# Carried-state and value-key products of an mLSTM kernel cut into tiles of 32 columns

## The chip, the core and the metric

One NeuronCore of one Trainium2 chip runs the whole program. Its engines are TensorE (PE, with its weight loads shown as PEld), VectorE (DVE), ScalarE (ACT), GpSimd (POOL) and the DMA queues, which SyncE (SP) starts. The metric is device microseconds (us) of one execution. The kernel before took 723.89 us, the median of three runs from 721.53 to 728.03.

## What is computed

The program is an mLSTM attention over 4 batches, 8 heads, 768 positions and 40 dimensions a head, and behind it two dense layers on the 3072 tokens. The attention keeps a state per head:

```python
for t in range(S):
    m_new = np.maximum(f_gate[:, :, t] + m, i_gate[:, :, t])
    f_stab = np.exp(f_gate[:, :, t] + m - m_new)
    i_stab = np.exp(i_gate[:, :, t] - m_new)
    C = f_stab[:, :, None, None] * C + i_stab[:, :, None, None] * np.einsum('bhd,bhe->bhde', vt, kt)
    n = f_stab[:, :, None] * n + i_stab[:, :, None] * kt
    h_tilde = np.einsum('bhde,bhe->bhd', C, qt)
    nq = np.einsum('bhd,bhd->bh', n, qt)[:, :, None]
    y[:, :, t] = o * h_tilde / np.maximum(np.abs(nq), 1.0)
```

Then `h = x @ w_in` with a softmax-weighted activation and a layer norm, `ln @ w_out`, and a gated layer of 1536 hidden units (`silu(x @ w_gate) * (x @ w_val) @ w_out`). All inputs and the output are float32.

## The kernel before

The attention is done in chunks of 128 positions (`L`). There are 6 chunks by 4 batches, 24 units `j`, and each unit holds all 8 heads. Within a chunk the products are matrix products; between chunks the state `C[b]` is carried, with the normaliser as a 41st column of each head (`D1` = 41). The 8 heads stand in the state in three groups of 3, 3 and 2: 120 partitions hold three heads' 40 key dimensions, and a mask keeps only the blocks that belong together.

Four products of a unit stand on TensorE, all in plain float32. The profile shows two records, a weight load and a matmul each, for every float32 matmul of the program:

- `sc` (line 405): queries by keys, 8 matmuls with 40 contraction rows, laid alternately in the upper and the lower half of the array's rows;
- `pv` (line 417): the masked scores by the values. Each head's 128 output rows are cut into four pieces of 32, so 32 matmuls of 32 weight columns and 41 moving columns;
- `pi` (line 424): the queries by the carried state, added to the same PSUM bank as `pv`: 3 matmuls with 120 contraction rows, 128 weight columns, and 123, 123 and 82 moving columns. It exists in 20 of 24 units (not in the first chunk);
- `pd` (line 432): the keys by the weighted values, 3 matmuls with 128 contraction rows, 120 weight columns and the same moving columns. It exists in 20 units (not in the last chunk). `cs` on VectorE masks its result, and `cd`/`ca` add it to the state.

Behind a unit's attention come, for its 128 tokens, `xT` (transposes, line 485), `h` (line 508), a softmax and a norm on VectorE and ScalarE, `uT` (transposes, line 554), `o` (line 571) and `x2` (transposes, line 485). The last layer follows (`gv`/`o2`, lines 749 to 794), from about 262 us to the end; in it a matmul uses 64 rows of the array.

Every engine executes its instructions in the order in which the program lists them. That order is written out by hand: the table `ORDER` names each step with its unit, as in `pv:8 ... pi:8`. So what stands before and behind each `pi` and `pd` on TensorE is fixed, and differs from unit to unit.

Of the kernel before, what the change touches and what calls it, by code (L numbers as in the profile page):

```python
# [19 lines left out]
L = 128  # L20
# [125 lines left out]
def kernel(  # L146
# [20 lines left out]
    D3 = 3 * D  # L167
    KF = FF // 128
    KF2 = w2.shape[0]
    act, dve, pool, pe, sp = nc.scalar, nc.vector, nc.gpsimd, nc.tensor, nc.sync  # L170
# [9 lines left out]
    def bank1():  # L180
        return psC.tile([128, 512], F32, tag="c", name="c")
# [47 lines left out]
    C, cols, gdr, edr, dend = {}, {}, {}, {}, {}  # L229
# [4 lines left out]
    def heads(a, p=128):  # L234
        return a[0:p, 0:H * D1].rearrange("p (h e) -> p h e", h=H)
# [184 lines left out]
    def pi(j):  # L420
        if j >= B:
            po, qt, b = T["pv", j], T["qT", j], j % B
            for g in range(3):
                pe.matmul(heads(po)[:, g::3, :], qt[:, g, :], C[b][:, g::3, :], start=False, stop=g == 2)  # L424

    def pd(j):
        kn = T["k", j]
        if j // B < NC - 1:
            pd_ = T["pd", j] = bank1()
            t = T["vw", j]  # L430
            for g in range(3):
                pe.matmul(heads(pd_, D3)[:, g::3, :], kn[:, g, :], t[:, g::3, :], start=True, stop=True)

    def th(j):
        T["th", j] = ak.tile([128, H, D], F32, tag="th", name="th", bufs=2)
# [538 lines left out]
```

## Time and profile before

| | |
|---|---|
| median of 3 runs | 723.89 us (721.53 to 728.03) |
| the profiled execution | 723.04 us |
| its span, first to last instruction | 721.0 us |
| TensorE busy | 696.8 us (97%) |
| VectorE busy | 450.2 us (62%) |
| ScalarE, GpSimd busy | 325.8 us (45%), 158.3 us (22%) |
| mean granted TensorE clock | 0.973 of full |

A matmul's busy time reaches from its start to the arrival of its result, so neighbours overlap, and a busy TensorE is not yet one at its peak. What an operation costs on a full TensorE is read from the distance between the start of its first record and the start of the next operation's first.

### The profile page before, as it was taken

To read this page: it belongs to the slowest core of one execution; us is meant where nothing else is said; L and a number is where in the kernel's file an instruction comes from. 1 tells how busy PE (TensorE), PEld (TensorE's weight loads), DVE (VectorE), ACT (ScalarE), POOL (GpSimd) and SP (SyncE) were. 2 spreads that over 40 slices of the span, in tenths; PEclk is the share of its full clock that TensorE was granted. 3 is DMA by queue.
4 is the path that set the end of the run, shared out by engine and by line. 5 is a ranking of instruction groups with operands and counts; after the bars stand their busy time and mean duration, and the time that the engine had idled before them with its cause. 6 is when DMAs were issued, how large, how long until landed. Compare 5 with 4: busy or idle time off the path is not lost.

```text
span 721.0 us, 16647 instructions
## 1 busy us (share of the span) xinstructions
PE 696.8 (97%) x7024; PEld 622.6 (86%) x7024; DVE 450.2 (62%) x765; ACT 325.8 (45%) x675; POOL 158.3 (22%) x230
## 2 busy tenths in 40 slices
PE   6898999999999999999999999999999999999997
PEld 6777888989999888888978888888888888888887
DVE  6999998867676696677997334344434443533433
ACT  4656757574746566567554322233222222323222
POOL 4555563624341112114235200000000000000000
PEclk8578999999999999999999999999999999999999
DMA  7897657544531042030430000010010001001001
GB/s 272 279 279 226 217 180 228 195 163 149 163 106 51 10 161 106 0 110 1 139 136 0 12 27 1 2 37 2 1 37 2 1 2 37 2 1 39 1 2 37
DMA packets 24011, 61.59 MB, mean 85 GB/s; under 512 B 3163, under 2 KB 11456, under 8 KB 23936
## 3 DMA queue, kind: packets, MB, share of 16 engines
q1 hardware_dynamic: 23936, 60.52, 26.1%
q8 instruction: 55, 0.90, 0.5%
q14 instruction: 20, 0.16, 0.1%
HBM read 56.40 MB, written 4.11 MB: 84 GB/s over the span
## 4 chain that ended last, share of the span: by engine, by line
PE 77%; DVE 11%; DMA 4%; ACT 3%; issue 2%; POOL 2%; SPq 0%; DVEq 0%; POOLq 0%; ACTq 0%
PE a L794 26%; PE c L794 14%; PE c L571 10%; PE a L508 9%; PE a L749 7%; PE c L779 3%; PE a L405 2%; PE a L554 2%; DMA kvo<-in_kvo_dram 2%; PE c L417 1%; PE c L485 1%; DVE e L521 1%; PE c L424 1%; DMA ed<-erow 1%; DMA W<-gd 1%
## 5 line engine op out<-in xcount | busy, mean ns | idle before, releaser
L794 PE MATMUL a<-Xh,w 64*128 64x512 f32 (+1 forms) x1100 | 180.2, 387 | 0.0
L757 DVE SCALAR_TENSOR_TENSOR t<-t,a 128x512 f32<-128x512 f32 x71 | 48.8, 688 | 142.6 <-ACT t L753 142.5
L794 PEld LDWEIGHTS a<-Xh,w 64*128 64x128 f32 x1100 | 101.1, 184 | 12.0 <-issue 0.2
L753 ACT ACTIVATE t<-a 128x512 f32<-128x512 f32 x71 | 42.4, 597 | 151.2 <-PE a L794 129.5
L794 PE MATMUL a<-Xl,w 64*128 64x512 f32 (+1 forms) x550 | 107.7, 382 | 0.0
L794 PE MATMUL c<-w,yh 64*128 64x320 f32 x896 | 100.5, 304 | 0.0
L794 PEld LDWEIGHTS c<-w,yh 64*128 64x128 f32 x896 | 81.4, 184 | 6.9
L765 ACT ACTIVATE yh<-t 128x512 fp32r<-128x512 f32 x71 | 44.8, 632 | 88.0 <-DVE t L761 86.8
L769 DVE TENSOR_TENSOR yl<-t,yh 128x512 fp32r<-128x512 f32 x63 | 44.7, 710 | 42.3 <-ACT yh L765 42.3
L794 PE MATMUL c<-w,yl 64*128 64x320 f32 x448 | 70.9, 306 | 0.0
L794 PEld LDWEIGHTS a<-Xl,w 64*128 64x128 f32 x550 | 53.6, 185 | 9.7
L571 PE MATMUL c<-wo_h,uh 128*128 128x320 f32 x192 | 60.9, 317 | 0.9 <-DVE dc L447 0.7
L749 PE MATMUL a<-Xh,w 128*128 128x512 f32 x180 | 59.0, 393 | 1.9 <-DVE t L761 1.4
L571 PE MATMUL c<-wo_h,ul 128*128 128x320 f32 x192 | 59.6, 311 | 0.3 <-DVE ul L562 0.3
L571 PE MATMUL c<-wo_l,uh 128*128 128x320 f32 x192 | 59.3, 309 | 0.0
L508 PE MATMUL a<-wi_h,xh 128*128 128x512 f32 x144 | 58.8, 408 | 0.0
L508 PE MATMUL a<-wi_h,xl 128*128 128x512 f32 x144 | 56.9, 395 | 1.0 <-DVE xl L497 1.0
L390 ACT ACTIVATE W<-W,col 128x128 f32<-128x128 f32 x176 | 53.5, 391 | 7.1 <-POOL W L380 7.1
L761 DVE SCALAR_TENSOR_TENSOR t<-t,a 128x512 f32<-128x512 f32 x71 | 48.7, 686 | 2.2
L794 PEld LDWEIGHTS c<-w,yl 64*128 64x128 f32 x448 | 43.5, 184 | 0.1
L749 PE MATMUL a<-Xl,w 128*128 128x512 f32 x108 | 42.1, 390 | 0.0
L562 DVE TENSOR_TENSOR ul<-a,uh 128x1024 fp32r<-128x1024 f32 x24 | 29.4, 1223 | 19.7 <-ACT uh L558 19.5
(146 smaller groups left out, 1320.4 us busy)
## 6 DMA issues: line engine op xcount, KB each, us to landing
kvo<-in_kvo_dram SPq DMA_DIRECT2D x24, 504.0 KB
rw<-in_w_dram SPq DMA_DIRECT2D x12, 960.0 KB
W<-gd SPq DMA_DIRECT2D x22, 512.0 KB
qk<-in_qkT_dram SPq DMA_DIRECT2D x48, 160.0 KB
out_dram<-ob SPq DMA_DIRECT2D x24, 160.0 KB
qT<-in_qx_dram SPq DMA_DIRECT2D x20, 180.0 KB
E<-ed SPq DMA_DIRECT2D x60, 60.0 KB
x2T<-in_w_in_dram SPq DMA_DIRECT2D x5, 512.0 KB
```

The lines of the kernel that those rows point to most:

```text
L390: act.activation(g[:, h, :], x[:, h, :], AF.Exp, bias=cols[c][:, b * H + h:b * H + h + 1])
L508: pe.matmul(ph[:, fs], x, w[:, fs], start=n == 0, stop=n == 7)
L562: dve.tensor_tensor(out=T["ul", j], in0=T["uT", j], in1=T["uh", j].bitcast(F32), op=ALU.subtract)
L571: pe.matmul(po[:, 0:DM], x[:, fs], w[:, f, :], start=n == 0, stop=n == 3 * KF - 1)
L749: pe.matmul(p[:, s * 512:s * 512 + GT], w, x, start=n == 0, stop=n == 7)
L753: act.activation(T["t", g, f], T["gv", g, f][:, 0:GT], AF.Tanh, scale=0.5)
L757: dve.scalar_tensor_tensor(out=t, in0=t, scalar=1.0, in1=p[:, 0:GT], op0=ALU.add, op1=ALU.mult)
L761: dve.scalar_tensor_tensor(out=t, in0=t, scalar=0.5, in1=p[:, 512:512 + GT], op0=ALU.mult, op1=ALU.mult)
L765: act.activation(T["yh", g, f], T["t", g, f], AF.Copy)
L769: alu[e].tensor_tensor(out=T["yl", g, f], in0=T["t", g, f], in1=T["yh", g, f].bitcast(F32), op=ALU.subtract)
L779: pe.matmul(T["acc", g][t][:, 0:DM], x[:, ts], w, start=f == 0 and n == 0, stop=f == KF2 - 1 and n == 2)
L794: i = T["last"] = pe.matmul(*args, **flags)
```

## The change

`pi` and `pd` are written with an inner loop over pieces of 32 output rows, as `pv` is. In `pi` the 128 weight columns become four pieces of 32; in `pd` the 120 become 32, 32, 32 and 24. Each matmul becomes four, with the same moving columns. Nothing else is changed; the order of the steps stays.

```diff
@@ def pi(j):
             for g in range(3):
-                pe.matmul(heads(po)[:, g::3, :], qt[:, g, :], C[b][:, g::3, :], start=False, stop=g == 2)
+                for t in range(0, L, 32):
+                    pe.matmul(heads(po)[t:t + 32, g::3, :], qt[:, g, t:t + 32], C[b][:, g::3, :],
+                              start=False, stop=g == 2)
@@ def pd(j):
             for g in range(3):
-                pe.matmul(heads(pd_, D3)[:, g::3, :], kn[:, g, :], t[:, g::3, :], start=True, stop=True)
+                for d in range(0, D3, 32):
+                    ds = slice(d, min(d + 32, D3))
+                    pe.matmul(heads(pd_, D3)[ds, g::3, :], kn[:, g, ds], t[:, g::3, :], start=True, stop=True)
```

Lines behind the first edit move by 2, behind the second by 4: `pi` is line 425 in the changed kernel, `pd` 436, the transposes 489 and 558.

On TensorE, a stretch in the middle of the attention (it runs from 113.8 to 119.5 us in the trace before). The names read output, then the two operands; `x8` is a count of like instructions. Before, one `pd` alone between transposes, then two units' `pv` and `pi`:

```order
L485 MATMUL c<-ident,x_1663 128x128 x3
L432 MATMUL c<-vw,kvo 120x3x41 x2
L432 MATMUL c<-vw,kvo 120x2x41
L554 MATMUL a<-ident,e 128x128 x8
L417 MATMUL c<-kvo,P 32x41 x32
L424 MATMUL c<-C_568,qT 128x3x41 x2
L424 MATMUL c<-C_568,qT 128x2x41
L485 MATMUL c<-ident,y 128x128 x3
L417 MATMUL c<-kvo,P 32x41 x32
L424 MATMUL c<-C_296,qT 128x3x41 x2
L424 MATMUL c<-C_296,qT 128x2x41
L405 MATMUL a<-qk 128x128 x8
```

And the same stretch after the change:

```order
L489 MATMUL c<-ident,x_1816 128x128 x3
L436 MATMUL c<-vw,kvo 32x3x41 x3
L436 MATMUL c<-vw,kvo 24x3x41
L436 MATMUL c<-vw,kvo 32x3x41 x3
L436 MATMUL c<-vw,kvo 24x3x41
L436 MATMUL c<-vw,kvo 32x2x41 x3
L436 MATMUL c<-vw,kvo 24x2x41
L558 MATMUL a<-ident,e 128x128 x8
L417 MATMUL c<-kvo,P 32x41 x32
L425 MATMUL c<-C_604,qT 32x3x41 x8
L425 MATMUL c<-C_604,qT 32x2x41 x4
L489 MATMUL c<-ident,y 128x128 x3
```

Nothing has changed places: 3 matmuls of `pi` are now 12 of 32 output rows, and 3 of `pd` are 9 of 32 and 3 of 24.

## Rows read from the trace of the kernel before

**Rows 1.** The page: TensorE and VectorE busy, and the chain by engine.
```profile
span 721.0 us, 16647 instructions
PE 696.8 (97%) x7024; PEld 622.6 (86%) x7024; DVE 450.2 (62%) x765; ACT 325.8 (45%) x675; POOL 158.3 (22%) x230
...
PE 77%; DVE 11%; DMA 4%; ACT 3%; issue 2%; POOL 2%; SPq 0%; DVEq 0%; POOLq 0%; ACTq 0%
```

**Rows 2.** Four stretches: busy us of each engine, granted clock, DMA share, GB/s.
```profile
12.00:44.00 32.00, 26.44 (x312) 22.69 (x313) 29.06 (x52) 19.46 (x56) 16.46 (x20) 0.52 0.91 285
44.00:105.00 61.00, 55.40 (x874) 48.45 (x872) 57.47 (x111) 39.15 (x104) 34.50 (x45) 0.94 0.73 216
105.00:262.00 157.00, 155.81 (x1874) 141.08 (x1874) 117.41 (x239) 94.38 (x219) 58.18 (x97) 1.00 0.45 144
262.00:721.00 459.00, 450.48 (x3911) 401.88 (x3908) 240.22 (x343) 168.23 (x287) 43.88 (x51) 1.00 0.09 29
```

**Rows 3.** The chain of waits, 40 to 110 us: start, us, what.
```profile
52.45 0.72 DVE wc L223
...
58.22 2.67 DVE wo_l L673 x2
...
62.91 1.21 DVE th L472
...
76.70 0.82 PE c L417 x64
77.52 0.83 PE c L424 x6
78.34 0.33 PE c L485 x3
...
99.78 1.22 DVE ul L562
```

**Rows 4.** TensorE's groups by line, 105 to 262 us: busy, mean ns, idle.
```profile
L424 PE MATMUL c<-C,qT 120*128 120x123 f32 (+1 forms) x78 | 11.3, 280 | 0.0
L417 PE MATMUL c<-kvo,P 128*32 128x41 f32 x832 | 10.6, 202 | 0.0
L432 PE MATMUL c<-vw,kvo 128*120 128x123 f32 (+1 forms) x60 | 7.8, 267 | 0.8 <-POOL vw L396 0.8
```

**Rows 5.** TensorE in time, 113.8 to 119.5 us: start, us, line, rows*columns, moving shape.
```profile
113.82 0.81 PE L485 MATMUL c<-ident,x 128*128 128x128 f32 x6
114.48 0.77 PE L432 MATMUL c<-vw,kvo 128*120 128x123 f32 x6
115.08 1.04 PE L554 MATMUL a<-ident,e 128*128 128x128 f32 x8
116.05 0.82 PE L417 MATMUL c<-kvo,P 128*32 128x41 f32 x64
116.79 0.90 PE L424 MATMUL c<-C,qT 120*128 120x123 f32 x6
117.53 0.49 PE L485 MATMUL c<-ident,y 128*128 128x128 f32 x3
117.95 0.82 PE L417 MATMUL c<-kvo,P 128*32 128x41 f32 x64
118.70 0.90 PE L424 MATMUL c<-C,qT 120*128 120x123 f32 x6
119.53 0.49 PE L405 MATMUL a<-qk 40*128 40x128 f32 x4
```

**Rows 6.** TensorE in time, a `pi` alone between transposes, and a `pv` before transposes.
```profile
156.40 0.80 PE L424 MATMUL c<-C,qT 120*128 120x123 f32 x6
157.04 0.60 PE L554 MATMUL a<-ident,e 128*128 128x128 f32 x4
...
216.89 0.82 PE L417 MATMUL c<-kvo,P 128*32 128x41 f32 x64
217.64 0.55 PE L485 MATMUL c<-ident,x 128*128 128x128 f32 x3
```

**Rows 7.** TensorE in time, the last two units of the attention.
```profile
248.86 0.49 PE L485 MATMUL c<-ident,x 128*128 128x128 f32 x3
249.18 0.49 PE L485 MATMUL c<-ident,y 128*128 128x128 f32 x3
249.60 0.82 PE L417 MATMUL c<-kvo,P 128*32 128x41 f32 x64
250.35 0.90 PE L424 MATMUL c<-C,qT 120*128 120x123 f32 x6
251.18 0.82 PE L417 MATMUL c<-kvo,P 128*32 128x41 f32 x64
251.93 0.90 PE L424 MATMUL c<-C,qT 120*128 120x123 f32 x6
252.62 0.39 PE L571 MATMUL c<-wo_h,uh 128*128 128x320 f32 x1
```

**Rows 8.** Weight loads of `pv` and `pi`: duration ns, least, median, most.
```profile
L417 PEld LDWEIGHTS c<-kvo,P x1536: 106/110/175, 20.7 to 251.8; 128*32 128x32 f32 x192
L424 PEld LDWEIGHTS c<-C,qT x120: 186/192/192, 53.6 to 252.5; 120*128 120x128 f32 x120
```

**Rows 9.** Who waited for `pd`, in us and times.
```profile
DVE dc L447: 1.4, 1
DVE C L444: 0.2, 1
```

## The prediction

> **What bounds the kernel.** First the page. TensorE is busy for 97% of the span, and the chain that ended last is 77% PE and 11% DVE [rows 1]. An average says little here, because the change touches only the attention, so I cut the span into stretches [rows 2]. From 12 to 44 us TensorE has 26.44 of 32 us and a granted clock of 0.52. From 44 to 105 us it has 55.40 of 61 and VectorE 57.47. From 105 to 262 us TensorE has 155.81 of 157, VectorE 117.41. After 262 us neither `pi` nor `pd` is left. The reader is to see that an operation made shorter on TensorE is paid out in the third stretch alone. The chain of waits says the same: between 52 and 75 us its pieces are VectorE's (`wc`, `wo_l`, `th`), the first `pv` and `pi` that stand on it together are those at 76.70 and 77.52, and near 100 us it is on VectorE again [rows 3]. So the sum is made for 105 to 262 us, and what comes before only widens the range.
>
> In that stretch `pi` has 78 records and `pd` 60 [rows 4]: six a unit, so 13 `pi` and 10 `pd`. All else is what these 23 operations cost before and after, from start to start.
>
> **What the rows show of 32-column tiles.** `pv` already runs in them. Its 64 records take 0.75 us to the start of `pi` [rows 7]; less the drain below, 0.66 us for 16 groups of four tiles, 41 ns a group. Three transposes take 0.32 us (248.86 to 249.18) [rows 7], 107 ns for 128 columns, so a record streams a column in two cycles at 2.4 GHz, and 41 columns need 34 ns. Four records in 41 ns, when one alone needs 34: the four tiles stream side by side, and the group costs 7 ns at most above one stream.
>
> **Bodies.** A `pi` alone between transposes takes 0.64 us from its start to the next [rows 6], a `pd` alone 0.60 [rows 5]. Streaming is less than that: 4 records of 123 columns and 2 of 82 make 4 x 103 + 2 x 68 = 548 ns. The rest is the load of 128 weight columns: the transposes load and stream 128 in 107 ns each, so the load sets the pace of records with fewer moving columns, the 82-column ones above all. After the change there are six groups of four tiles (three heads, three heads, two heads, two passes each). With half of the 7 ns on each, 4 x 106 + 2 x 72 = 568 ns. Bounds: 548 (streams alone), and 41/34 of that, 660 ns, if a group stretches as its stream does. If I took the whole 0.75 us over 16 groups, 47 ns, it would be 750. I take 0.57 us, nearest to the row that has four tiles in steady state. So 13 x -0.07 and 10 x -0.03: **-1.2 us**.
>
> **Changes of tiling.** Three transposes take 0.42 us before `pv` (249.18 to 249.60) against 0.32 before their like [rows 7]: entering the 32-column tiles costs 0.10. A `pi` behind `pv` takes 0.74 us to the transposes [rows 5] against 0.64 alone [rows 6]: its first weight load isn't hidden, 0.10 more. A `pi` before the next `pv` or before `sc` takes 0.83 (250.35 to 251.18, 118.70 to 119.53) [rows 5, 7]: 0.09 again, the array running empty before another tiling. The Trainium skill, page "TensorEngine Tiling (Array Packing)", section "Key Properties", says that switching the tiling mode drains TensorE. By that the trace agrees, with 0.09 us each; were it not so, the term of +0.8 below would be 0.
>
> What does the change do to the number of switches? In the order of instructions from 105 us on, `sc` is one tiling, the 32-column operations another, all the rest the third. Before there are 46 switches; after, with `pi` and `pd` in the tiling of `pv`, 55. `pv` and `pi` now run into each other, but a `pd` or `pi` that stands alone, as the `pd` at 114.48, has two switches that it had not. Nine more at 0.09: **+0.8**.
>
> First weight loads: 9 `pi` and 1 `pd` stand right behind a `pv` and lose the 0.10, **-1.0**. Exits from the 32-column tiles to other work rise from 3 to 17. There the first load is only partly visible: three transposes behind `pv` span 0.55 us instead of 0.49 [rows 5, 6]. 14 x 0.05: **+0.7**. Entering has the load of 32 columns, some 0.01 for each of five more entries: +0.1. Weight loads themselves take 110 ns instead of 192 at the median [rows 8], beside other work.
>
> Sum: -1.2 + 0.8 - 1.0 + 0.7 + 0.1 = **-0.6 us**. By blocks it looks so: `pv`, `pi`, transposes -0.1; `pv`, `pi`, `sc` -0.26 (0.09 + 0.83 becomes 0.57 + 0.09); a lone `pd` +0.2 (0.60 becomes 0.10 + 0.57 + 0.09 + 0.05); the last four operations -0.5 [rows 7]. From the 0.02 by which I rounded each of these, the sum may as well be -1.0. The `pv` and `pi` at 76.70 on the chain add -0.1.
>
> The profiled execution took 723.04 us for its span of 721.0, and lies 0.85 below the median. 723.04 - 0.8 = 722.2; from the median it would be 723.1. I forecast **722.6 us**.
>
> **What else the edits touch.** No wait is added and no DMA moved. The records of the 23 operations rise from 138 to 552, each with a weight load; `pv` issues 64 in 0.75 us [rows 7], so 24 in 0.57 are no load for the queue. A lone `pd` ends some 0.1 us later, and `cs` on VectorE behind it; those waits were 1.4 and 0.2 us in all [rows 9], and VectorE has 39 us to spare in the stretch [rows 2].
>
> **Rivals.**
>
> *The bodies don't shrink.* The same page, section "When to Use Tiling", gives column tiling to products whose output side or moving side is small; neither pass of `pi` is, with 128 weight columns. As a mechanism here: 128 columns fill the array either way, the streams are as long as before, and only the switches count. For it: 548 of 640 ns are streaming, which tiles can't cut. Against it: the weight load's part can go, and `pv` shows its tiles' loads hidden. Time: -1.2 falls away, +0.6, 723.6 us. Chance 0.2.
>
> *The long streams hinder each other, slower than before.* `pv` shows four streams of 41 columns, none of 123. If a group takes the 47 ns of `pv`'s whole share for each 41 columns, a body takes 0.75: 13 x 0.11 + 10 x 0.15 = +2.9, and with the switches +3.5: 726.5 us. It decides from the group time at which bodies and switches cancel: body gain 0.6 over 23, 0.026 each, a body of 0.60, thus 112 ns for a group of three heads instead of 106. Chance 0.13.
>
> *The tiles don't overlap at all*, or the fourth tile of `pd`, 24 columns wide, is taken for another tiling. Without overlap a body is 4 x 0.55 = 2.2 us, +1.6 each, 23 of them +37: 760 us. With a switch at each 24-wide tile, 12 a `pd` (in and out, three times, two passes), 10 x 12 x 0.09 = +11: 734 us. Against it: `sc` has 40 rows and runs as the array's halves, and `pv`'s overlap. Chance 0.06.
>
> *Far faster.* All 40 operations on the path, with the early ones at half the clock (0.52 granted [rows 2]), and their switches gone: at most twice the stretch's saving for the 17 others, about -3: 719.5 us, still within 1%. For more the start would have to reorder itself behind VectorE and the DMAs. Chance 0.05 for over 1%.
>
> **Numbers.** The forecast, -0.6 to -1.0 with its like, has 0.56. Low end: 719.5, less 1 us for the spread of runs, 718.5. High end: 726.5 and 1.5 for the spread (the runs before reach to 728.03), 728. What a measurement of this kernel can tell from no change is about 1%, 7 us. Faster by more 0.05; slower by more 0.06, the third rival, and 0.01 for what I don't see; within 1% the rest, 0.88.
>
> **What would show it.** Right: on the changed kernel's timeline a `pi` behind `pv` starts some 0.02 us after `pv`'s last record, with 24 records, and the block `pv`, `pi`, `sc` shrinks by 0.26; a lone `pd` takes 0.66 to 0.7 from start to start, and the transposes before it 0.10 more. Wrong: a body of over 0.60 (second rival), or gaps within `pd` at its 24-wide tiles (third). The last `pi` should end, against the start of the last layer, as before, and the stretch from 105 to 262 us be 0.6 to 1.0 us shorter; if the whole moves by more, look before 105 us, where VectorE's chain and the clock decide.

## The result and the profile after

The changed kernel takes 725.98 us (median of 20 runs, 722.87 to 732.08), the kernel before 721.82 us (20 runs, 718.93 to 728.03): a ratio of 1.0058, interval 1.0039 to 1.0077. It is slower by about 4 us where I had forecast 0.6 to 1.3 us less. The base has moved too: twenty runs put the kernel before 2 us under the median of three that the forecast used. The profiled execution took 724.07 us, span 721.8.

First the page of the changed kernel: span and engines, and the DMA queue that carries instructions (queue, kind: packets, MB, share).

```profile
span 721.8 us, 18087 instructions
PE 696.2 (96%) x7744; PEld 618.2 (86%) x7744; DVE 444.6 (62%) x765; ACT 325.9 (45%) x675; POOL 157.3 (22%) x230
...
q8 instruction: 60, 0.98, 0.6%
```

Beside [rows 1] there are 720 more matmuls and as many weight loads. Before, the instruction queue had 55 packets and 0.90 MB. With all instructions of TensorE counted in the traces (14,124 before, 15,564 after) a packet of 16 KB holds some 257 to 259 of them by division; that the step is 256 is borne out below.

Next TensorE in time, the stretch that answers to [rows 5] (start, us, line, rows*columns, moving shape):

```profile
115.66 0.78 PE L436 MATMUL c<-vw,kvo 128*32 128x123 f32 x24
116.36 1.09 PE L558 MATMUL a<-ident,e 128*128 128x128 f32 x8
117.39 0.82 PE L417 MATMUL c<-kvo,P 128*32 128x41 f32 x64
118.01 0.76 PE L425 MATMUL c<-C,qT 120*32 120x123 f32 x24
118.71 0.55 PE L489 MATMUL c<-ident,y 128*128 128x128 f32 x3
119.19 0.82 PE L417 MATMUL c<-kvo,P 128*32 128x41 f32 x64
119.81 0.76 PE L425 MATMUL c<-C,qT 120*32 120x123 f32 x24
120.50 0.71 PE L405 MATMUL a<-qk 40*128 40x128 f32 x8
```

This is what the prediction had reckoned. The lone `pd` takes 0.70 from start to start (forecast 0.66 to 0.70). `pv`, `pi`, `sc` take 1.31 us from `pv` to `sc` (119.19 to 120.50); in [rows 5] it was 1.58, so -0.27 for the forecast's -0.26. `pv` and `pi` to the transposes: 1.32 for 1.48, and the transposes span 0.55.

But 18 us earlier the same engine stands still in the middle of a `pi`. Same view, 96.5 to 105 us:

```profile
96.57 0.78 PE L425 MATMUL c<-C,qT 120*32 120x123 f32 x24
97.17 0.79 PE L417 MATMUL c<-kvo,P 128*32 128x41 f32 x63
97.76 0.27 PE L425 MATMUL c<-C,qT 120*32 120x123 f32 x1
97.78 0.20 PE L417 MATMUL c<-kvo,P 128*32 128x41 f32 x1
97.78 0.39 PE L425 MATMUL c<-C,qT 120*32 120x123 f32 x5
100.91 0.61 PE L425 MATMUL c<-C,qT 120*32 120x123 f32 x16 [2.73 <-issue]
...
104.55 0.63 PE L575 MATMUL c<-wo_h,uh 128*128 128x320 f32 x1
```

The brackets say how long TensorE was idle and what ended it: 2.73 us, and "issue", which is time in which it waited for nothing that the profile shows. No semaphore stands on the next weight load. In the kernel before the same `pi`, `pd` and `sc` run through, and only `o` behind them waits, for VectorE:

```profile
101.11 0.82 PE L417 MATMUL c<-kvo,P 128*32 128x41 f32 x64
101.86 0.90 PE L424 MATMUL c<-C,qT 120*128 120x123 f32 x6
102.59 0.80 PE L432 MATMUL c<-vw,kvo 128*120 128x123 f32 x6
103.32 1.16 PE L405 MATMUL a<-qk 40*128 40x128 f32 x16
105.23 0.41 PE L571 MATMUL c<-wo_h,uh 128*128 128x320 f32 x1 [0.75 <-DVE dc L447]
```

That wait of 0.75 us is gone after the change, so not the whole pause is added time. A second pause stands after the last `pi`, in the middle of `o`:

```profile
252.53 0.31 PE L575 MATMUL c<-wo_h,ul 128*128 128x320 f32 x1
253.80 0.41 PE L575 MATMUL c<-wo_h,uh 128*128 128x320 f32 x1 [0.96 <-issue]
```

The kernel before has no wait of TensorE's matmuls that ends in "issue". The first pause has a second price, in the granted clock (stretch, its length, busy us of PE, PEld, DVE, ACT, POOL, granted clock, DMA share, GB/s):

```profile
98.00:100.00 2.00, 0.17 (x6) 0.00 (x0) 1.97 (x4) 2.00 (x9) 0.92 (x2) 1.00 0.63 175
100.00:102.00 2.00, 1.09 (x40) 1.10 (x41) 0.35 (x2) 0.38 (x2) 0.26 (x1) 0.93 0.50 149
102.00:104.00 2.00, 2.00 (x24) 1.71 (x18) 1.32 (x4) 0.00 (x0) 1.19 (x2) 0.50 0.04 10
...
106.00:108.00 2.00, 2.00 (x9) 2.00 (x9) 1.89 (x9) 1.70 (x6) 0.00 (x0) 0.50 0.57 151
```

Behind it the clock stands at its lower level (0.50 of 2.4 GHz) until about 108 us: TensorE had been idle from 98.2 to 100.9. The `o` at 104.55 takes 5.5 us, and 3.7 in the kernel before.

Counting TensorE's instructions in the trace, the first as number 0, the one after the first pause is number 3009 = 11 x 256 + 193, the one after the second 7617 = 29 x 256 + 193. Both are 449 behind a multiple of 256, which is 63 short of 512, two packets.

### The profile page after: what moved, and what is told of

Same layout as the page of the kernel before. It is cut to its first block, busy times and chain, and to the rows that moved or that the text cites. A ratio compares the mean times of both kernels' runs of the same rounds, so it can differ in the third digit from the quotient of the medians.

```text
span 721.8 us, 18087 instructions
## 1 busy us (share of the span) xinstructions
PE 696.2 (96%) x7744; PEld 618.2 (86%) x7744; DVE 444.6 (62%) x765; ACT 325.9 (45%) x675; POOL 157.3 (22%) x230
## 4 chain that ended last, share of the span: by engine, by line
PE 82%; DVE 11%; ACT 3%; DMA 2%; issue 2%; SPq 1%; DVEq 0%; ACTq 0%
PE a L798 26%; PE c L798 14%; PE c L575 11%; PE a L512 10%; PE a L753 7%; PE a L405 3%; PE c L783 3%; PE a L558 3%; PE c L489 2%; PE c L417 2%; PE c L425 1%; DMA qk<-in_qkT_dram 1%; PE c L436 1%; DVE P L409 1%; DVE cc L223 1%
```

## Experiments

**Theory A, instruction supply.** The theory takes it that the next packet is asked for some 128 instructions into a packet and is usable several us later. (In the trace after, from 297 to 710 us, where the pace is even, packets start when TensorE stands 153 to 186 behind a multiple of 256.) Before, `pv` with its 128 instructions in 0.63 us was followed by slower work. Now `pi`, `pv`, `pi`, `pd` in a row are 272 instructions, in some 2.4 us at the full clock and without a pause (an estimate: four operations of about 0.6 us each). Where a packet's boundary falls badly, TensorE runs out. **Theory B**: only bodies and switches count, the pauses are accidents. **Theory C**: the 32-column tiles themselves pull the clock down. Which instruction begins a packet can be shifted without touching the work: a few matmuls whose results nobody uses, near 10 us, where TensorE waits anyway.

Ten `pi` and two `pd`, those beside a `pv`, cut (`grp`):

```diff
+CUT_PI = (11, 12, 13, 14, 16, 18, 19, 21, 22, 23,)
+CUT_PD = (13, 18,)
@@ def pi(j):
-                for t in range(0, L, 32):
+                w = 32 if j in CUT_PI else L
+                for t in range(0, L, w):
@@ def pd(j):
-                for d in range(0, D3, 32):
+                w = 32 if j in CUT_PD else D3
+                for d in range(0, D3, w):
```

> Ten units' pi and two units' pd are cut into 32-column tiles, those that stand beside a pv (or beside one that is cut); all others stay whole. Theory A (instruction supply): TensorE's instructions come in pieces of 16 KB, 256 instructions; in the changed kernel both long pauses of TensorE without a semaphore stand 449 instructions behind a multiple of 256. The next piece is asked for about 128 instructions into the one before, and is usable 4 to 6 us later; 320 instructions that run in less leave TensorE without any. By the order and the starts before, this kernel has two such stretches, 2.9 us near 119 us and 2.7 us near 252 us: two pauses of 1 to 3 us there with no semaphore, and the saving of 1.9 us by bodies and switches is lost: 0 to +3 us against the kernel before. Theory B (bodies and switches alone): -1.9 us, no such pause. Theory C (the clock falls because the tiles occupy the array less): the granted clock falls below 1.0 behind the cut operations near 119 and 252 us without a pause ahead of it.

The same with padding (in the order table `wp:40` behind `gb:0`):

```diff
+    def wp(n):
+        p = bank1()
+        for i in range(n):
+            t = i % 4 * 32
+            pe.matmul(p[t:t + 32, 0:D1], ident[:, t:t + 32], ident[:, 0:D1], start=True, stop=True)
```

> The same tiles as the run beside it, and 40 further matmuls of 32 by 41 columns (160 instructions, results unused) near 10 us, where TensorE waits for the first values anyway. They only shift which instruction begins a piece of 256. Theory A: the fastest stretches of 320 instructions from 128 behind a multiple of 256 are now 7.2 us (near 151 and 124 us), so there is no pause near 119 or 252 us, and the saving is paid out: -1.5 to -2 us against before, 2 to 5 us under the run beside it. Theory B: as the run beside it, -1.9, the padding costing at most 0.5. Theory C: as the run beside it.

Measured on the same chip, against the same runs of the kernel before (723.87 us): without padding 724.34 us, 1.0015 (0.9990 to 1.0039); with padding 721.62 us, **0.9957 (0.9933 to 0.9981)**. Only the phase differs (which instruction begins a packet), and the 160 useless instructions ahead. TensorE in time, without padding:

```profile
117.96 0.61 PE L428 MATMUL c<-C,qT 120*32 120x123 f32 x15
119.22 0.43 PE L428 MATMUL c<-C,qT 120*32 120x123 f32 x9 [0.65 <-issue]
...
250.15 0.72 PE L428 MATMUL c<-C,qT 120*32 120x123 f32 x18
252.43 0.34 PE L428 MATMUL c<-C,qT 120*32 120x82 f32 x5 [1.56 <-issue]
```

The pauses stand at the two places that the expectation names, both 449 behind a multiple of 256. With padding the same work runs through:

```profile
119.00 0.76 PE L428 MATMUL c<-C,qT 120*32 120x123 f32 x24
119.69 0.55 PE L493 MATMUL c<-ident,y 128*128 128x128 f32 x3
120.17 0.82 PE L419 MATMUL c<-kvo,P 128*32 128x41 f32 x64
120.80 0.76 PE L428 MATMUL c<-C,qT 120*32 120x123 f32 x24
121.49 1.16 PE L407 MATMUL a<-qk 40*128 40x128 f32 x16
...
251.87 0.77 PE L428 MATMUL c<-C,qT 120*32 120x123 f32 x23
252.57 0.42 PE L579 MATMUL c<-wo_h,uh 128*128 128x320 f32 x1
```

Theories B and C fall: the tiles are the same in both, and the granted clock of both was 1.00 from 97 to 262 us.

The control, the kernel before with the same padding (the hunk above alone):

> The kernel before with the same 40 further matmuls, a control. Its fastest stretch of 320 instructions is then 5.9 us near 253 us, beside 5.1 us near 104 us without padding. All theories: within 0.5 us of the kernel before, no pause without a semaphore of over 1 us; Theory A allows a short one near 253 us.

724.39 us, 1.0008 (0.9984 to 1.0032), no pause: the padding is not what helped.

The changed kernel with 24 padding matmuls:

> The changed kernel with 24 such matmuls (96 instructions) at the same place. Theory A: the pauses near 98 and 252 us are gone; new ones stand near 117.8 us (a stretch of 3.0 us) and 150.3 us (2.8 us), each 1 to 3 us, and the instruction that pauses is again 449 behind a multiple of 256; time as the changed kernel's, +1 to +5 against before. Theory B: no pauses of its own, the time is the changed kernel's. Theory C: the clock falls near 102 us again, whatever the padding.

723.60 us, 1.0006 (0.9983 to 1.0030), less than expected. The pauses moved to where they were expected, near 117 and 150 us, each 449 behind a multiple of 256, and were short; near 99 us 0.20 us was left, at the same position:

```profile
118.01 0.38 PE L405 MATMUL a<-qk 40*128 40x128 f32 x3 [0.77 <-issue]
...
151.21 0.36 PE L417 MATMUL c<-kvo,P 128*32 128x41 f32 x16 [0.46 <-issue]
```

Each part alone (the other's inner loop has one piece, `w = D3` or `w = L`):

> Only pi is cut, in all 20 units; pd is whole. Bodies and switches from 105 us on: -0.8 us, with the stretch from 75 us -1.1. Theory A (instruction supply): the fastest stretches of 320 instructions, from 128 behind a multiple of 256, are 2.9 us (near 119 us), 3.1 us (near 252 us) and 4.9 us (near 104 us): pauses of 0.5 to 2.5 us without a semaphore at the first two, 449 instructions behind a multiple of 256; 0 to +3 us against the kernel before. Theory B (bodies and switches alone): -0.8 to -1.1, no pause.

> Only pd is cut, in all 20 units; pi is whole. It stands between work of other tilings nearly everywhere. Theory B, and Theory A alike for this part: bodies 10 x -0.035 and eleven more switches, +1.0 us from 105 us on. Theory A: the fastest stretch of 320 instructions is 4.6 us near 152 us, where TensorE waits later anyway, the next 5.1: no pause of over 0.5 us. Time +0.5 to +1.5 by both.

Only `pi`: 728.91 us, 1.0087 (1.0051 to 1.0123), more than expected. Three pauses stand in its trace, 1.16 us near 103, 0.65 near 119 and 1.49 near 251, all at position 449; behind 262 us its trace is 3.7 us longer than that of the kernel before, among other things by a wait of 2.5 us for VectorE near 370 us (1.4 in the kernel before) and a granted clock of 0.51 from 372 to 374 us behind it. What delays VectorE there is open. Only `pd`: 725.58 us, 1.0040 (1.0009 to 1.0070). Its one pause is 0.51 us near 104 us, and a lone `pd` between work of another tiling costs 0.2 us more, as reckoned. The time is 2.6 us over that of before, more than the 0.5 to 1.5 expected, with an interval from 0.7 to 5.1; the table below shows none of it from 97.6 to 262 us, so the rest stays open.

More units cut, chosen by the order so that no fast stretch falls on a packet's end:

```diff
+CUT_PI = (4, 5, 6, 7, 8, 9, 10, 11, 12, 13, 14, 16, 18, 21, 22, 23,)
+CUT_PD = (5, 6, 7, 8, 13, 14, 15, 18,)
```

> pi is cut in units 4 to 14, 16, 18 and 21 to 23, pd in units 5 to 8, 13 to 15 and 18: those that stand in a row with a pv; with 4 padding matmuls (16 instructions) near 10 us. Chosen so that no stretch of 320 instructions from 128 behind a multiple of 256 takes under 6.5 us. Theory A: no pause; bodies and switches pay -1.9 us from 105 us on and up to -3.3 with the work ahead of it: -2 to -3 us against before. Theory B: the same, with no part in it for the phase. Under the run with ten pi and two pd by 0 to 1 us.

720.88 us, 0.9977 (0.9952 to 1.0002): not the -2 to -3 us of the expectation, and not told from no change. Two pauses of 0.58 and 0.51 us came near 104 and 152 us at position 449. TensorE went on 7.0 and 7.3 us behind instruction 128, so the 320 instructions themselves had taken 6.4 and 6.8 us. In the padded `grp`, 6.8 us near 125 us passed without a pause. So the packet's delay is no constant.

The opposite way: the kernel before, with `pi` and `pd` whole, and two units' `pv` made of twice as many instructions.

```diff
-            for t in range(0, L, 32):
-                pe.matmul(po[t:t + 32, h * D1:(h + 1) * D1], P[:, h, t:t + 32], vn[:, h, :],
-                          start=h == 0, stop=j < B and h == H - 1)
+            for lo, hi in ((0, 20), (20, D1)) if j in (22, 23) else ((0, D1),):
+                for t in range(0, L, 32):
+                    pe.matmul(po[t:t + 32, h * D1 + lo:h * D1 + hi], P[:, h, t:t + 32], vn[:, h, lo:hi],
+                              start=h == 0 and lo == 0, stop=j < B and h == H - 1)
```

> The kernel before, pi and pd whole; in the last two units' pv (units 23 and 22) each matmul is cut along its 41 moving columns into 20 and 21, the same products with twice the instructions: 256 instead of 128 a unit. The pv's body should grow by at most 0.2 us, since 20 columns stream in 17 ns and a group's four pieces start 7 ns apart. Theory A: the stretch from 128 to 449 behind a multiple of 256 near 251.6 us is run in 1.7 us, so TensorE pauses there for 2 to 4 us without a semaphore, 449 instructions behind a multiple of 256, although neither pi nor pd is cut; +2 to +4 us. Theory B: +0.3 at most, no pause. Theory C (the clock by the tiles): no fall of the clock, for the tiles and products are those of before.

```profile
250.19 0.94 PE L418 MATMUL c<-kvo,P 128*32 128x20 f32 x89
252.42 0.53 PE L418 MATMUL c<-kvo,P 128*32 128x21 f32 x39 [1.28 <-issue]
```

725.30 us, 1.0049 (1.0023 to 1.0076), with one pause, at position 449. It needs neither cut `pi` nor cut `pd`, only many instructions in a short time. It was shorter than the 2 to 4 us expected, while the time rose by about the expected 2 to 4: the two `pv` also took 0.46 and 0.66 us longer to the start of the `pi` behind them, pause taken out (the first 248.16 to 249.37, 0.75 in the kernel before), where the expectation had 0.2 us at most. Pause and bodies make the whole 2.4 us by which the four operations from the first of these `pv` to `o` are longer (5.41 us for 3.02 in [rows 7]).

At last the kernels themselves once more:

> The changed kernel once more, for a second trace. Theory A (instruction supply): pauses without a semaphore again near 98 and 252 us, 449 instructions behind a multiple of 256, of 0.5 to 3 us each; where one is over 2 us the granted clock falls behind it. Theory B (bodies and switches alone): no pause, the first trace's were accidents.

> The changed kernel a third time. As the run beside it: Theory A has both pauses again, of another length; Theory B none.

> The kernel before once more. Its fastest stretches of 320 instructions are 5.1 us near 104 us and 5.9 us near 122 us. Theory A: no pause, or one of under 1 us near 104 us. It also tells how far the stretch from 105 to 262 us and the clock behind 262 us differ between two executions of one kernel: the first trace has a wait of 0.8 us near 160 us that the padded control did not have.

> The kernel with ten pi, two pd and the padding once more. Theory A: no pause of over 0.5 us again; the stretch from 105 to 262 us 1.5 to 2.5 us shorter than that of the kernel before beside it.

They give single executions (722.97 and 726.22 us; 721.61, with another of the kernel before at 725.16; 722.00), and their traces say what the medians don't. In both of the changed kernel's, both pauses are there again, at the same two instructions; the longer one, of each:

```profile
99.13 0.40 PE L425 MATMUL c<-C,qT 120*32 120x123 f32 x5
101.41 0.31 PE L425 MATMUL c<-C,qT 120*32 120x123 f32 x4 [1.88 <-issue]
```

```profile
102.70 0.39 PE L425 MATMUL c<-C,qT 120*32 120x123 f32 x5
104.35 0.61 PE L425 MATMUL c<-C,qT 120*32 120x123 f32 x16 [1.25 <-issue]
```

The clock did not fall behind these (1.00 from 97 to 112 us in both traces); the first trace had the long one. The padded `grp` had no pause again. All traces together, from the start of `uT` at 97.61 us in the trace before to that of `o` at 262.41, the same two instructions in each:

| kernel | pauses (us) | this stretch (us) |
|---|---|---|
| before; once more; padded | none; none; none | 164.8; 163.9; 163.9 |
| after; again; third | 2.73 + 0.96; 1.88 + 0.63; 1.25 + 0.96 | 169.4; 165.5; 165.0 |
| after, 24 padding matmuls | 0.20 + 0.77 + 0.46 | 164.6 |
| ten `pi`, two `pd` | 0.65 + 1.56 | 165.4 |
| the same, padded; once more | none; none | 162.4; 162.5 |
| more units | 0.58 + 0.51 | 162.6 |
| only `pi`; only `pd` | 1.16 + 0.65 + 1.49; 0.51 | 166.3; 164.7 |
| `pv` in twice as many instructions | 1.28 | 166.5 |

## Why the prediction was wrong

The **bounds** held in the stretch from 105 to 262 us: there TensorE's time is the kernel's. But the longer pause stands at 98 to 101 us, ahead of that stretch, of which the prediction had said that it "only widens the range".

The **bodies** and **changes of tiling** held block by block, as shown above. The padded `grp`, where nothing else comes in, gains 1.4 to 2.4 us in the stretch against the three traces of before; 1.9 had been reckoned for it, and 1.5 at least for its second trace, which is 1.4 under the second of before. One small slip in the prediction's sum: five more entries at 0.01 make 0.05, not 0.1.

The step that failed is in "What else the edits touch": that `pv` issues 64 records in 0.75 us, so that 24 in 0.57 are no load for the queue. It put the supply of instructions at nothing. A single `pi` is none. But I compared one operation with one operation, where the limit is on 320 instructions in a row, and the change lays `pv` (128 instructions) and `pi` and `pd` (48 each, 12 before) side by side. Before, the fastest such stretch from 128 to 449 behind a multiple of 256 took 5.1 us (near 104 us); after, 3.2 us near 98 and 3.0 us near 252, the pauses taken out. In all fourteen traces, up to 262 us, pauses again taken out, every one of the 13 such stretches that ran in under 4 us (2.4 to 3.4) ended in a pause, as did 5 of the 25 that took 4.3 to 6.9 us, and none that took longer. The rivals looked for harm in the streams and in the switches, none in the supply of instructions. The sign of the forecast turned on it: pauses of 2.2 to 3.7 us an execution, and in one of three a fall of the clock, against a gain of about 1 us.

Theory A is shown for the pauses: every one of them, 18 in nine traces, stands 449 instructions behind a multiple of 256; they move with the padding; and they can be made in the kernel before. The packets' own times in the traces say it most directly. Each of the 18 pauses ends 1.3 to 1.6 us after an instruction packet has landed, and that packet had started 2.2 to 2.8 us before the end; the packet before it had landed at least 7.9 us before. (The 2.73 us: packet from 98.33 to 99.40 us, first weight load at 100.90.) What varies lies ahead of the packet's start, which came 1.1 to 4.9 us behind instruction 128; what sets that is open. The Trainium skill, page "Runtime: NRT & Kernel Launch", section "Instruction fetch mechanics", has refills in blocks of 256 instructions, with which the trace agrees (60 packets, 0.98 MB). It also holds the fetch to be hidden behind the pace of issue; here the measurement differs, with up to 2.73 us in the open, and decides.

The size is shown in part. In the stretch of the table the three traces after average 166.6 us, the three of before 164.2: +2.4 us, of the 2.8 to 5.6 that the interval of the ratio gives on 722 us. Three traces against three, with lengths of the pause from 1.25 to 2.73 us, can't say whether long pauses in other executions make up the rest. Two figures on record point that way. The changed kernel with 24 padding matmuls has the same tiles, pauses of 1.4 us in all, and a ratio of 1.0006 (0.9983 to 1.0030) instead of 1.0058 (1.0039 to 1.0077), though on another chip. And the granted clock, averaged over executions, is 0.971 in the 20 runs of the changed kernel and 0.974 in the 67 of the kernel before in the experiments: an estimate of 2 us from 0.003 of 722, but where in the execution it was lost the runs don't tell. Ahead of 97.6 us the traces of one kernel differ by 2 to 5 us among themselves, so nothing can be read there.

That 725.98 lies inside the forecast's range of 718.5 to 728 is luck. The second rival's number (726.5), which had set the high end, came out near the time and for another reason; its group time of 112 ns was not reached, since a body between `pv` and `pv` takes 0.57 us (250.25 to 250.82 in the changed kernel).

## What to carry to other kernels

Before cutting TensorE work into more and shorter matmuls, count the instructions of the densest few microseconds, neighbours included, as well as the cost of each operation: here 320 in under 4 us left the engine waiting each time. An idle entry "issue" in the middle of an operation, with no semaphore on the next instruction, is the sign, and its position in the instruction stream, modulo 256, the test. Cut only those operations that stand beside others of the same tiling, and if a pause remains, look at where the packet boundaries fall: `grp` was 0.4% faster with 160 useless instructions ahead of it.

## What was unexpected

A pause of 2.73 us was followed by some 6 us at half the clock; pauses of 1.25 and 1.88 us in the same place, and of 1.56 elsewhere, were not. The wait of 2.5 us for VectorE in the kernel with only `pi` cut was, by some 3 us at about half.

Behind 262 us, where the two kernels have the same work, nine of fourteen traces have 1.7 us more or, with only `pi` cut, 3.7; the kernel before, in its second trace, is among them. In the padded control it is a wait for ScalarE that the first traces of neither kernel have:

```profile
393.47 0.31 PE L785 MATMUL c<-w,yl 128*128 128x320 f32 x1
394.87 0.55 PE L785 MATMUL c<-w,yh 128*128 128x320 f32 x2 [1.09 <-ACT yh L771]
```

What delays ScalarE there is open. It moves single executions by nearly half as much as this change did, so a pair of profiles must be compared up to 262 us, and whole times by many runs.
